# Threshold offsets in another PSUM buffer, accumulation matmuls split 4, 6, 2, scaling and proposals over other steps, 14 idle matmuls at the start

## The chip, the core and the metric

The kernel runs on one core of a Trainium2 chip. Times are device microseconds (us) of one launch, inputs and outputs in HBM. PE is the matrix engine, DVE, ACT and POOL are the vector, scalar and GpSimd engines, SP issues most DMAs. Smaller is better.

## The reference, cut to what matters

Capped attention over 8 batches, 12 heads, 448 positions, 64 channels, then a mixture of 8 experts in which tokens are given out greedily in the order of their logits, at most 448 to an expert and one expert to a token.

```python
scores = cap * np.tanh(scale * (q @ k.T) / cap)
attn = np.exp(scores - max); attn /= attn.sum(-1)
x = (attn @ v)                       # 3584 tokens of 768
flat = (x @ w_gate).flatten()        # 3584 x 8 logits
for idx in np.argsort(-flat):        # greedy, capacity 448
    tok, e = idx // 8, idx % 8
    if assigned[tok] >= 0 or counts[e] >= 448: continue
    assigned[tok] = e; counts[e] += 1
out[mask_e] = np.maximum(x[mask_e] @ w1[e], 0) @ w2[e]
```

## The kernel before, in words

**Attention** (`attention`, from line 22). Heads are worked on four at a time: 24 groups `g`, three to a batch, `b, m = divmod(g, 3)`. Step `g` computes the scores of group `g` in seven rounds of matmuls (`qk`, line 157; line 152 in the first and last group) into `psS`, of which there are two buffers. ACT takes the tanh of each (line 158) and, two or three rounds together, the exponential (line 163). In between, PE multiplies the exponentials of group `g-1` with the values (`avq`, line 197) into two buffers `psA`, which DVE copies to `xT` (`av_out`, line 218) before the next group may use them. DVE also adds the exponentials up (`esum`, line 168: four instructions a group, `et` and `es`).

The sums over positions and the gate logits of batch `bb = b-1` are accumulated one batch later by twelve small matmuls (`rnd`, line 228). Each writes 32 of the 128 partitions of one PSUM buffer, and `R[x]` says which 32 (`k`) and from what: in the order of `R`, entries 0 to 3, 4 to 7 and 8 to 11 each hold the four values of `k` once. Five of them are issued in step m=0, five in m=1, two in m=2; for batch 0 the two sums of group 0 take two matmuls each.

After the last two (m=2) DVE copies the result (`logit_in`, line 244), PE transposes it (line 250), and DVE turns it into logits (lines 265 to 270). In the last batch (b=7) the transposes (`logit(bb)`) stand right behind the copy, in front of the fifth round of scores; in the others they stand at the end of the step. `turn2` (line 235) transposes `xT` into `Y` on DVE; two batches later `inv` (line 241) and `scale` (line 35, two halves of 1344 columns) normalise `Y`, and `put` (line 32) writes it out. `propose` (lines 474 to 505, on DVE) prepares the search from the logits of two batches at a time: twelve small operations (`propose_a`) and six (`propose_b`).

Within attention PE, ACT, DVE and SP do their instructions in the order in which the code issues them; a wait stops all that stands behind it on the same engine.

**The first search** (`search`, `select`). The 448 best tokens of the first expert are found by 16 threshold steps in three runs, A (5), B (6) and C (5). A step compares all values with three thresholds, one on ACT (line 538) and two on DVE, adds the counts up by a small matmul (line 550), and picks the next threshold (line 554, `fl` and `t0`). From a run's second step on (`quick`) DVE's compare (line 542) adds the distance of the thresholds to `t0` itself; that distance is an operand in PSUM, `s.cps`, which lies in columns 128 and up of `psX`. Columns 0 to 127 of the same buffer are the target of idle matmuls (`warm`, line 786), whose result nobody reads: PE gets two, one or five of them behind each step's small matmul, and, in some steps, also a transpose of the last batch's output (line 40) or a part of the last group's product (line 209).

A tile's readers wait for its writers through semaphores that the framework places by tile.

**The experts** (`ffn_all`). From 360 us PE multiplies the gathered tokens with both weight matrices of expert after expert (lines 951 and 1013) until 834 us, with hardly a gap.

At the very start (lines 68 to 74) ACT's queue issues the load of the single number `cap`, half of the first group's `q`, and `cap` for all partitions (`capt`, from which DVE makes the `bias` of the exponential); PE does four idle matmuls.

Of the kernel before, what the change touches and what calls it, by code (L numbers as in the profile page):

```python
# [6 lines left out]
F32=mybir.dt.float32; F32R=mybir.dt.float32r; BF16=mybir.dt.bfloat16; F16=mybir.dt.float16; I32=mybir.dt.int32; I16=mybir.dt.int16  # L7
AF=mybir.ActivationFunctionType; ALU=mybir.AluOpType; AX=mybir.AxisListType
# [10 lines left out]
def attention(nc, tc, c1, xp, yp, ep, nv, pM, q, k, v, vl, cap, w_gate, xs, L1, ident, on_logits, on_turn, setup, mark):  # L19
# [11 lines left out]
    def put(b):  # L31
        for c in range(4): nc.sync.dma_start(rows(b)[:,c*W:c*W+W].rearrange("(k s) c -> s k c",s=32),Y[b][c*32:c*32+32].rearrange("p k n d -> p k (n d)"))
    def scale(b,i,eng):
        w=slice(i*NB//2,(i+1)*NB//2)
        eng.tensor_tensor(Y[b][:,w],Y[b][:,w],sm[b][:,w].unsqueeze(3).broadcast_to([128,NB//2,NP,32]),op=ALU.mult)
# [13 lines left out]
    with ExitStack() as ctx:  # L49
# [8 lines left out]
        def load(g,part,lo=0,hi=HG*S,eng=None):  # L58
            if g>=N: return
            if part==2:  # L60
                vz=nv.tile([128,7*HG*D],F32,name="nv")
                nc.sync.dma_start(vz,v[g])
                nats[g,2]=vz.rearrange("p (r h d) -> p r h d",r=7,h=HG) if whole(g) else (vz[:,:6*HG*D].rearrange("p (j h d) -> p j h d",j=3,d=D),vz[:,6*HG*D:].rearrange("p (h d) -> p h d",d=D))
                return
            if lo==0: tks[g,part]=tp.tile([128,HG,S],F32,name="t"+"kq"[part])
            (eng or nc.sync).dma_start(tks[g,part].rearrange("p m s -> p (m s)")[:,lo:hi],(k,q)[part][g][:,lo:hi])
        cap1=c1.tile([1,1],F32,name="cap1"); capt=c1.tile([128,1],F32,name="capt")
        nc.scalar.dma_start(cap1,cap)
        for part in range(2): load(0,part,0,S,(nc.sync,nc.scalar)[part])
        nc.scalar.dma_start(capt,cap.broadcast_to([128,1]))  # L70
        tb=c1.tile([128,1],F32,name="tb")
        nc.vector.memset(tb,0.0); nc.scalar.activation(tb,tb,AF.Tanh)
        ps=pM.tile([128,512],F32,name="psM")
        for _ in range(4): nc.tensor.matmul(ps[:,:128],ident,ident,start=True,stop=True)

        ones=c2.tile([128,NQ,HG,32],F32,name="ones")
        nc.gpsimd.memset(ones,0.0)
# [88 lines left out]
        def esum(g,what):  # L166
            if not 0<=g<N: return
            add=lambda o,a,b: nc.vector.tensor_tensor(o,a,b,op=ALU.add)  # L168
            if g==0:
                if what=='e1': es_t[g]=es.tile([128,2,2,S],F32,name="es0",bufs=1)  # L170
                t=es_t[g]
                if what in ('e1','e2'):
                    o=int(what[1])-1
                    add(t[:,o],ex(g,o,0),ex(g,o,1)); add(t[:,o],t[:,o],ex(g,o,2))
                else:
                    e=ev(g,6)
                    for o in range(2):
                        w=slice(64*(1-o),128-64*o)
                        add(t[w,o],t[w,o],e[w])
                return  # L180
            if what=='e1': et[g]=es.tile([128,2,2,S],F32,name="et",bufs=2)
            t=et[g]
            if what=='e1': add(t,eh[g,0],eh[g,1])
            if what=='e2': add(t,t,eh[g,2][:,0:2])
            if what=='r':
                es_t[g]=es.tile([128,2,S],F32,name="es",bufs=5)
                add(es_t[g],t[:,0],t[:,1]); add(es_t[g],es_t[g],ev(g,6))
        avp={}
        def avq(g,j,x):
# [50 lines left out]
            for c in range(4): nc.gpsimd.tensor_copy(sm[b][c*32:c*32+32],t[c//2*96:c//2*96+32,:,c//2*16:c//2*16+NP])  # L240
        def inv(b): nc.vector.reciprocal(sm[b],sm[b])
        def logit_in(b):
            lgs[b]=lgt[b]=xp.tile([128,S],F32,name="lg",bufs=1)
            nc.vector.tensor_copy(lgs[b],misc.pop(b)[:,:S])
        def logit(b,part=None,some=False,pool=None):
            if b not in lgs: logit_in(b)
# [45 lines left out]
        for g in range(N):  # L292
            b,m=divmod(g,NQ); bb=b-1
            for z in LD.get(g,()): load(int(z[0]),int(z[1]))
            if g>2:
                load(g+1,2); load(g+2,0); load(g+2,1)
            if g==2: gates()
            last=g==N-1
            if g==N-8: vload()
            if g==N-5: vgate()  # L300
            if g==N-3: vback()
            qk(g,0); qk(g,1)
            turn2(g-2)
            if b>1:
                if m==0: inv(b-2)
                if m<2: scale(b-2,m,nc.vector)
                if m==1: put(b-2)
            order=g>0; head=0<g<4
            for j in range(1 if head else 2 if order else 3): avq(g-1,j,0)
            if head: qk(g,2); avq(g-1,1,0)  # L310
            for w in ('e2','r'): esum(g-1,w)
            if not head: qk(g,2)
            if order: avq(g-1,2,0)
            if m==2 and b: rnd(bb,10,12)
            qk(g,3)
            if order: qk(g,4)
            if m==0 and b: rnd(bb,0,5)
            if m==1 and bb>=0:
                rnd(bb,5,10)
                if bb>0: on_logits(bb-1)  # L320
            if m==2 and bb>0: on_turn(bb-1)
            if m==2 and b: logit_in(bb)
            if m==2 and b==B-1: logit(bb)
            if order: qk(g,5)
            else: qk(g,4)
            avq(g-1,0,1)
            if head: qk(g,6)
            avq(g-1,1,1)
            if not order: qk(g,5); avq(g-1,2,1)
            if not head: qk(g,6)  # L330
            if order: avq(g-1,2,1)
            avq(g-1,3,1)
            if not last: esum(g,'e1')
            if g: av_out(g-1,0); av_out(g-1,1)
            if m==2 and 0<b<B-1: logit(bb)
            if m==2 and bb>=0: turnsum(bb)
        g=N-1; b=B-1
        rnd(b,0,8,8)
        logit_in(b)
        inv(b-1)  # L340
        vround(0); vround(1)
        part=logit(b,some=True,pool=pT)
        vround(2); vround(3)
        lgs[b]=xp.tile([128,S],F32,name="lg",bufs=1); ps=misc.pop(B)
        nc.vector.tensor_copy(lgs[b],ps[:,:S])
        ps=pT.tile([128,512],F32,name="psA")
        av(g,0,3,ps,3,2)
        logit(b,part)
        for j in range(3): av(g,0,j,ps,3,2)
    avs=[lambda ps,j=j: av(N-1,1,j,ps,0,3) for j in range(4)]  # L350
# [3 lines left out]
    return [lambda pool,i=i: lambda: held(i) for i in range(2)]+[lambda pool,p=p: xt(B-1,p,pool) for p in range(NP)],avs  # L354


YL=[]; YB=2
LK=(0,0,112,112,112,112,112,112); FT=2
ACF=1
LF=1  # L360
# [3 lines left out]
class Routing:  # L364
# [160 lines left out]
    def select(s,wp,Vt,ab,mid=None,post=None):  # L525
# [6 lines left out]
        for i in range(steps):  # L532
# [3 lines left out]
            with nc.allow_low_precision(reason="integers up to 256 are exact in bfloat16"):  # L536
                quick=s.cur==0 and i>0
                for k in [0] if quick else range(na,m): nc.scalar.activation(o,Vt,AF.Sign,bias=th[k],scale=-1.0,accum_out=cd[:,k:k+1])
                for k in range(1,m) if quick else range(na):
                    o=wp.tile([128,NV],BF16,name="cmpD",bufs=2)  # L540
                    if quick:
                        v.scalar_tensor_tensor(o,Vt[:,:NV],t0,s.cps[ab][:,i,k:k+1].broadcast_to([128,NV]),op0=ALU.subtract,op1=ALU.is_lt,accum_out=cd[:,k:k+1])  # L542
                        continue
                    with s.tc.issue_after(s.hold) if s.hold else nullcontext(): v.tensor_scalar(o,Vt[:,:NV],th[k],None,op0=ALU.is_lt,op1=ALU.add,accum_out=cd[:,k:k+1])  # L544
            if quick: v.tensor_scalar(H[:,i,m:2*m],C[:,i,0:m],t0,None,op0=ALU.add,op1=ALU.add,accum_out=wp.tile([128,1],F32,name="nt",bufs=2))
# [18 lines left out]
    def search(s,wp,turned=()):  # L564
        nc=s.nc; v=nc.vector
        post=None
        if s.cur==0:
            ps=s.spare(); s.cps={}; o=128
            for n in "ABC":
                S=s.steps[n]; s.cps[n]=ps[:,o:o+3*S].rearrange("p (s k) -> p s k",k=3); o+=3*S  # L570
                nc.scalar.activation(s.cps[n][:,1:],s.C[n][:,1:],AF.Copy)
        if turned:
            for h in range(s.NC//16):
                if ("VA",h) not in turned: s.turn("VA",h)
            late=[lambda: s.propose_b(s.NC-4,s.NC,PB(nc))]
            post=lambda: s.flips(s.pm.tile([128,512],F32,name="psM"))
        else: late,post=s.turns()
        yield 5
        yield from s.select(wp,s.V["VA"],"A",late,post)
# [157 lines left out]
def ffn_all(nc, tc, ctx, rt, xs, xz, yb, wg, w1, w2, out, ident, E, wp, deferred, xctx, gen, avs):  # L737
# [53 lines left out]
    while len(res)<1:  # L791
        step()
        if rt.pos=='B':
            warm(2 if UN[m] else 1 if m in AN else 5)
            if m in AN:
                put=avs.pop(0)(pa)
                if put: late.append(put)
            units(UN[m%len(UN)]); m+=1
        elif rt.pos=='A': posts()
# [285 lines left out]
def full(nc,tc,q,k,v,vl,cap,wg,w1,w2,out):  # L1085
    with ExitStack() as ctx:
# [3 lines left out]
        xz=[dr.tile([n,768],I16,name=f"xz{i}") for i,n in enumerate((512,384))]  # L1090
        yb=dr.tile([448,768],F32,name="yb")
        ident=cp.tile([128,128],F32,name="ident"); make_identity(nc,ident)
        cp.tile([128,64],F32,name="pad")
        L1=cp.tile([112,32,8],F32,name="L1")
        r=Routing(nc,cp,3584,8); r.ident=ident; r.tc=tc
        xctx=ExitStack()
# [1 line left out]
        xp=xctx.enter_context(tc.tile_pool(name="xp",bufs=2,side="right"))  # L1098
        yp=xctx.enter_context(tc.tile_pool(name="yp",bufs=YB,side="right"))
        ep=xctx.enter_context(tc.tile_pool(name="ep",bufs=2,side="right"))  # L1100
        nv=xctx.enter_context(tc.tile_pool(name="nv",bufs=5,side="right"))
        pM=xctx.enter_context(tc.tile_pool(name="pM",bufs=2,space=PSUM,side="right"))
        r.psum=lambda: pM.tile([128,512],F32,name="psM")
        turned=set()
        def on_logits(b):
            if b%2 or b==6: (r.propose if b<7 else r.propose_a)(L1,4*b-(4 if b<6 else 0),4*b+4)
        def on_turn(b):
            if b==3:
                r.turn("VA",b//4); turned.add(("VA",b//4))
        r.mark=[None]  # L1110
# [59 lines left out]
```

## Time and profile before

| what | us |
|---|---|
| three runs: median (lowest to highest) | 857.3 (856.39 to 859.15) |
| the profiled execution's own time | 856.05 |
| its span, first to last instruction | 854.3 |
| PE busy in the span | 827.7 (97%) |
| DVE, ACT, POOL busy | 595.3, 567.4, 392.5 |
| share of the last chain on PE, ACT, DVE | 87%, 6%, 2% |

The span is divided by what runs: attention to about 313 us, search and gather to about 360, the experts after that. PE's share of the chain is high in all of them, so the question in each stretch is which instruction PE waited for last, and what stood between two of its instructions. In a row of the timeline, square brackets give the idle time of the engine just before the row and who ended it.

### The profile page before, as it was taken

Reading aid. Unit: us, or ns where it says so; the run is one execution under the profiler, and the core shown is the slowest. Engines: PE = TensorE matmul, PEld = TensorE weight load, DVE = VectorE, ACT = ScalarE, POOL = GpSimd, SP = SyncE. Lnnn points to the kernel's source line nnn. Section 1 sums busy time; section 2 is a strip of 40 time slices with the busy share of each in tenths; the row PEclk is TensorE's granted clock in tenths of the full one; section 3 lists DMA queues with packets and bytes.
Section 4 is the critical chain, followed back from the end, with each engine's and each line's share of the span. In section 5 each row is a group of like instructions: output and inputs, shape, how many; then the busy total and the mean of one; then the engine's idle time right before and its main releaser. Section 6 shows DMA issues by size and latency. Waiting matters only on the chain.

```text
span 854.3 us, 16156 instructions
## 1 busy us (share of the span) xinstructions
PE 827.7 (97%) x5720; PEld 574.4 (67%) x5720; DVE 595.3 (70%) x1913; ACT 567.4 (66%) x747; POOL 392.5 (46%) x585
## 2 busy tenths in 40 slices
PE   6999999999999997899999999999999999999996
PEld 2333333333333435688888888888888899999996
DVE  2667889879888976777887977878868874352210
ACT  7999999999999964284393593665655755544500
POOL 7600000000000015284387497596486687786843
PEclk9999999999999999999999999999999999999999
DMA  6323536355654305360764886977967968958714
GB/s 232 116 108 130 146 115 194 109 153 156 190 116 145 66 1 130 121 241 17 271 204 134 250 281 220 288 233 220 278 220 216 298 207 242 335 185 259 241 65 130
DMA packets 116003, 155.10 MB, mean 182 GB/s; under 512 B 66962, under 2 KB 80498, under 8 KB 115922
## 3 DMA queue, kind: packets, MB, share of 16 engines
q1 hardware_dynamic: 108208, 124.73, 48.5%
q0 software_dynamic: 4832, 22.03, 7.6%
q10 hardware_dynamic: 2882, 7.31, 2.2%
q8 instruction: 45, 0.74, 0.4%
q14 instruction: 36, 0.29, 0.1%
HBM read 105.18 MB, written 40.60 MB: 171 GB/s over the span
## 4 chain that ended last, share of the span: by engine, by line
PE 87%; ACT 6%; DVE 2%; DMA 1%; issue 1%; POOL 1%; SPq 0%; ACTq 0%; DVEq 0%; POOLq 0%
PE psH L951 28%; PE psH L1013 25%; PE psA L197 12%; PE psS L157 12%; ACT e L158 3%; PE psM L228 3%; ACT e L163 3%; PE psX L786 2%; PE psS L152 1%; DVE cmpD L542 1%; POOL out_dram L971 1%; DVE cmpD L544 1%; PE psR L550 1%; DMA on<-yb 1%; PE psM L250 1%
## 5 line engine op out<-in xcount | busy, mean ns | idle before, releaser
L1013 PE MATMUL psH<-hh,w2h 128*128 128x448 f32 x720 | 199.2, 367 | 0.0
L158 ACT ACTIVATE e<-psS 128x896 f32<-128x896 f32 x168 | 148.0, 912 | 21.7 <-PE psS L157 17.2
L163 ACT ACTIVATE e<-e,bias 128x1792 f32<-128x1792 f32 (+2 forms) x74 | 147.1, 1990 | 0.9
L157 PE MATMUL psS<-tq,tk 64*64 64x448 f32 x1248 | 140.4, 544 | 5.7 <-ACT e L158 5.5
L951 PE MATMUL psH<-xgh,w1h 128*128 128x448 f32 (+1 forms) x384 | 141.7, 369 | 0.3 <-ACT xgh L901 0.2
L1013 PEld LDWEIGHTS psH<-hh,w2h 128*128 128x128 f32 x720 | 134.1, 188 | 8.9 <-DVE hh L961 0.6
L951 PE MATMUL psH<-xgh,w1l 128*128 128x448 f32 (+1 forms) x384 | 139.8, 364 | 0.0
L829 POOL TENSOR_TENSOR w1l<-w1r,w1h 128x768 fp32r<-128x768 f32 x62 | 115.3, 1861 | 51.6 <-ACT w1h L822 46.2
L951 PE MATMUL psH<-xgl,w1h 128*128 128x448 f32 (+1 forms) x384 | 135.6, 366 | 0.0
L829 POOL TENSOR_TENSOR w2l<-w2r,w2h 128x768 fp32r<-128x768 f32 x64 | 132.1, 2066 | 6.2 <-ACT w2h L822 4.6
L197 PE MATMUL psA<-e,nv 64*64 64x448 f32 x1232 | 132.2, 536 | 0.0
L240 POOL COPY sm<-lgt 32x84 f32<-32x84 f32 x28 | 6.9, 247 | 264.9 <-DVE lgt L238 264.1
L1013 PE MATMUL psH<-hh,w2l 128*128 128x448 f32 x360 | 124.3, 367 | 0.0
L157 PEld LDWEIGHTS psS<-tq,tk 64*64 64x64 f32 x1248 | 43.1, 132 | 85.2 <-ACT e L158 42.5
L197 PEld LDWEIGHTS psA<-e,nv 64*64 64x64 f32 x1232 | 48.6, 133 | 67.6 <-issue 64.9
L822 ACT ACTIVATE w2h<-w2r 128x768 fp32r<-128x768 f32 x64 | 76.6, 1210 | 0.3 <-DMA w2r<-in_moe_w_dram 0.2
L951 PEld LDWEIGHTS psH<-xgh,w1h 128*128 128x128 f32 x384 | 72.4, 189 | 5.7 <-ACT xgh L901 0.9
L951 PEld LDWEIGHTS psH<-xgh,w1l 128*128 128x128 f32 x384 | 72.2, 188 | 4.5
L951 PEld LDWEIGHTS psH<-xgl,w1h 128*128 128x128 f32 x384 | 72.2, 188 | 4.3 <-DVE xgl L913 0.2
L1013 PEld LDWEIGHTS psH<-hh,w2l 128*128 128x128 f32 x360 | 67.6, 188 | 4.3
L168 DVE TENSOR_TENSOR et<-e,e 128x1792 f32<-128x1792 f32 x22 | 44.5, 2022 | 34.9 <-ACT e L163 34.9
L960 ACT ACTIVATE hh<-psH 128x448 fp32r<-128x448 f32 x56 | 30.1, 538 | 58.1 <-PE psH L951 55.5
(395 smaller groups left out, 1280.6 us busy)
## 6 DMA issues: line engine op xcount, KB each, us to landing
w1r<-in_moe_w_dram SPq DMA_DIRECT2D x64, 384.0 KB, 4.8
w2r<-in_moe_w_dram SPq DMA_DIRECT2D x64, 384.0 KB, 5.6
nv<-in_v_dram SPq DMA_DIRECT2D x24, 448.0 KB, 5.6
tk<-in_k_dram SPq DMA_DIRECT2D x23, 448.0 KB, 3.4
tq<-in_q_dram SPq DMA_DIRECT2D x23, 448.0 KB, 4.7
yb<-yq SPq DMA_DIRECT2D x60, 168.0 KB, 3.8
xs<-Y SPq DMA_DIRECT2D x28, 336.0 KB, 5.8
on<-yb SPq DMA_DIRECT2D x7, 1152.0 KB
```

Of the source, the lines that this page charges most:

```text
L157: nc.tensor.matmul(ps[w:w+64,h,:S],tks[g,0][hp,o,r*64:r*64+64],tks[g,1][hp,o,:],start=True,stop=True)
L158: nc.scalar.activation(ev(g,r),ps[:,:,:S],AF.Tanh,scale=sr[0])
L163: act=lambda: nc.scalar.activation(e,e,AF.Exp,scale=sr[1],bias=bias)
L168: add=lambda o,a,b: nc.vector.tensor_tensor(o,a,b,op=ALU.add)
L197: for h in range(2): nc.tensor.matmul(avp[g,o][h*64:h*64+64,:S],z[w,r,h,:],ev(g,r)[w,h,:],start=r==0,stop=r==6)
L228: nc.tensor.matmul(ps[k*32:k*32+32,:S],lhs,rhs,start=x<4 and i==0,stop=x==max(y for y in range(end) if R[y][0]==k))
L786: for _ in range(n): nc.tensor.matmul(t[:,:128*w].rearrange("p (w c) -> p w c",w=w),ident,ident.unsqueeze(1).broadcast_to([128,w,128]),sta ...
L822: nc.scalar.activation(view(h),r,AF.Copy)
L829: (eng or nc.gpsimd).tensor_tensor(view(l),r,view(h).bitcast(F32),op=ALU.subtract)
L951: nc.tensor.matmul(ps[:,o:C],a[:,c,:],b[:,c,o:],start=(m==0 and o==0),stop=(m==DC*3-1)); m+=1
L960: nc.scalar.activation(h,ps[:,:C],AF.Relu)
L1013: nc.tensor.matmul(ps[:,:C],spl[p,2,hf,f//2][w][:,f%2,cc*128:cc*128+128],h[a][:,f],start=(m==0),stop=(m==nm-1))
```

## The change

Nine edits, all in the order and place of work; what is computed stays.

```diff
+        for part in range(2): load(0,part,0,S,(nc.sync,nc.scalar)[part])
         nc.scalar.dma_start(cap1,cap)
-        for part in range(2): load(0,part,0,S,(nc.sync,nc.scalar)[part])
...
-        for _ in range(4): nc.tensor.matmul(ps[:,:128],ident,ident,start=True,stop=True)
+        for _ in range(14): nc.tensor.matmul(ps[:,:128],ident,ident,start=True,stop=True)
...
                 if m==0: inv(b-2)
-                if m<2: scale(b-2,m,nc.vector)
-                if m==1: put(b-2)
+                if m: scale(b-2,m-1,nc.vector)
+                if m==2: put(b-2)
...
-            if m==0 and b: rnd(bb,0,5)
+            if m==0 and b: rnd(bb,0,4)
             if m==1 and bb>=0:
-                rnd(bb,5,10)
+                rnd(bb,4,10)
...
-            if m==2 and bb>=0: turnsum(bb)
+            if m==2 and 0<=bb<B-2: turnsum(bb)
...
         logit_in(b)
-        inv(b-1)
+        turnsum(b-1)
...
         av(g,0,3,ps,3,2)
+        inv(b-1)
...
-                        v.scalar_tensor_tensor(o,Vt[:,:NV],t0,s.cps[ab][:,i,k:k+1].broadcast_to([128,NV]),op0=ALU.subtract,op1=ALU.is_lt,accum_out=cd[:,k:k+1])
+                        v.scalar_tensor_tensor(o,Vt[:,:NV],t0,s.cps[ab][:,i-1,k-1:k].broadcast_to([128,NV]),op0=ALU.subtract,op1=ALU.is_lt,accum_out=cd[:,k:k+1])
...
-            ps=s.spare(); s.cps={}; o=128
+            ps=s.pm.tile([128,512],F32,name="psM"); s.cps={}; o=480
             for n in "ABC":
-                S=s.steps[n]; s.cps[n]=ps[:,o:o+3*S].rearrange("p (s k) -> p s k",k=3); o+=3*S
-                nc.scalar.activation(s.cps[n][:,1:],s.C[n][:,1:],AF.Copy)
+                S=s.steps[n]-1; s.cps[n]=ps[:,o:o+2*S].rearrange("p (s k) -> p s k",k=2); o+=2*S
+                nc.scalar.activation(s.cps[n],s.C[n][:,1:,1:],AF.Copy)
...
-            post=lambda: s.flips(s.pm.tile([128,512],F32,name="psM"))
+            post=lambda: s.flips(ps)
...
-            warm(2 if UN[m] else 1 if m in AN else 5)
+            warm(2 if UN[m] else 1 if m in AN else 4)
...
         def on_logits(b):
-            if b%2 or b==6: (r.propose if b<7 else r.propose_a)(L1,4*b-(4 if b<6 else 0),4*b+4)
+            if b%2 or b==6: r.propose_a(L1,4*b-(4 if b<6 else 0),4*b+4)
+            if b==6: r.propose_b(4*b,4*b+4)
         def on_turn(b):
+            if b%2 and b<6: r.propose_b(4*b-4,4*b+4)
```

The number of buffers follows: `Y` 2 to 3, `lg` 1 to 2, `es` 5 to 4, `nv` 5 to 4, and a pad is 8 columns smaller. `on_logits(bb-1)` is called in step m=1, `on_turn(bb-1)` in m=2.

On PE, the accumulation matmuls of one batch (steps m=0 and m=1 of a middle batch; `xT,gw` are gate entries, `es,ones` sums) stand like this before:

```order
L157 MATMUL psS<-tq,tk 64x448 x8
L228 MATMUL psM<-xT,gw 32x448 x2
L228 MATMUL psM<-es,ones 32x448 x2
L228 MATMUL psM<-xT,gw 32x448
L157 MATMUL psS<-tq,tk 64x448 x4
...
L228 MATMUL psM<-xT,gw 32x448
L228 MATMUL psM<-es,ones 32x448 x4
```

The five of m=0 stand together, and five of m=1 behind them. After the change the same place reads:

```order
L157 MATMUL psS<-tq,tk 64x448 x8
L228 MATMUL psM<-xT,gw 32x448 x2
L228 MATMUL psM<-es,ones 32x448 x2
L157 MATMUL psS<-tq,tk 64x448 x4
...
L228 MATMUL psM<-xT,gw 32x448 x2
L228 MATMUL psM<-es,ones 32x448 x4
```

The fifth small matmul has moved from the step m=0 to the step m=1, where it is the first of six.

On DVE, the last group (step 23, b=7, m=2), from the copies of `psA` to the copy `lg` for which PE's transposes wait, before:

```order
L218 COPY xT<-psA 128x448 x2
L168 TENSOR_TENSOR et<-et,e_2759 128x1792
L168 TENSOR_TENSOR es<-et 128x896
L168 TENSOR_TENSOR es<-es,e_2759 128x896
L244 COPY lg<-psM 128x448
```

Between the copies of `psA` and the copy `lg` there are three additions. After the change:

```order
L218 COPY xT<-psA 128x448 x2
L35 TENSOR_TENSOR Y<-Y,sm 128x1344
L168 TENSOR_TENSOR et<-et,e_2763 128x1792
L168 TENSOR_TENSOR es<-et 128x896
L168 TENSOR_TENSOR es<-es,e_2763 128x896
L493 TENSOR_SCALAR r_Bt<-r_b 112x8
...
L505 SCALAR_TENSOR_TENSOR r_K_348<-r_kk,r_Ct 112x8
L244 COPY lg<-psM 128x448
```

One half of a scaling (L35) and the six operations of `propose_b` now stand in front of that copy. In the other third groups they are added in the same place.

## Rows read from the trace of the kernel before

**Rows 1.** Windows of the span: each engine's busy time, granted clock, DMA share, GB/s

```profile
100.00:283.00 183.00, 181.73 (x1787) 66.62 (x1783) 156.25 (x187) 170.53 (x145) 4.94 (x20) 1.00 0.50 147
336.40:346.20 9.80, 6.30 (x52) 5.56 (x52) 5.06 (x37) 3.24 (x9) 1.08 (x2) 1.00 0.43 140
346.20:350.00 3.80, 3.80 (x20) 3.80 (x21) 2.42 (x15) 0.00 (x0) 0.00 (x0) 0.55 0.00 0
360.00:834.00 474.00, 473.38 (x2496) 424.29 (x2496) 315.77 (x1408) 264.22 (x451) 329.71 (x354) 1.00 0.70 221
```

**Rows 2.** Chain that ended last, one batch: start us, us, what

```profile
199.43 1.62 PE psM L228 x10
```

**Rows 3.** Timeline of PE, same batch: start, us, instruction, idle before

```profile
185.04 0.95 PE L228 MATMUL psM<-xT,gw 128*32 128x448 f32 x4
...
200.98 0.98 PE L157 MATMUL psS<-tq,tk 64*64 64x448 f32 x8
```

**Rows 4.** Timeline of ACT, same batch

```profile
199.74 1.72 ACT L158 ACTIVATE e<-psS 128x896 f32<-128x896 f32 x2
...
204.29 0.92 ACT L158 ACTIVATE e<-psS 128x896 f32<-128x896 f32 x1 [0.35 <-PE psS L157]
```

**Rows 5.** Timeline of DVE, a first, second and third group

```profile
190.40 2.02 DVE L168 TENSOR_TENSOR et<-e,e 128x1792 f32<-128x1792 f32 x1 [2.88 <-ACT e L163]
...
208.08 1.52 DVE L35 TENSOR_TENSOR Y<-Y,sm 128x1344 f32<-128x1344 f32 x1
...
215.40 0.17 DVE L492 TENSOR_SCALAR r_Bt<-r_b 112x8 f16<-112x8 int32 x1
...
216.04 2.02 DVE L168 TENSOR_TENSOR et<-e,e 128x1792 f32<-128x1792 f32 x1
```

**Rows 6.** Timeline of the last group, DVE and PE

```profile
294.63 1.15 DVE L218 COPY xT<-psA 128x448 f32<-128x448 f32 x2
...
296.65 2.02 DVE L168 TENSOR_TENSOR et<-et,e 128x1792 f32<-128x1792 f32 x1 [0.87 <-ACT e L163]
...
300.85 0.62 DVE L244 COPY lg<-psM 128x448 f32<-128x448 f32 x1
...
301.68 0.65 PE L250 MATMUL psM<-ident,lg 128*112 128x128 f32 x4
```

**Rows 7.** Line 542: what its engine waited for, us and times

```profile
  PE psX L786: 6.7, 13
```

**Rows 8.** Timeline of the first search, DVE and PE

```profile
327.22 0.97 PE L209 MATMUL psX<-e,nv 128*64 128x448 f32 x4
327.33 0.45 DVE L542 SCALAR_TENSOR_TENSOR cmpD<-r_qt,th,psX 128x224 bf16<-128x224 f16 x1 [0.16 <-PE psX L786]
...
332.06 0.45 DVE L542 SCALAR_TENSOR_TENSOR cmpD<-r_qt,th,psX 128x224 bf16<-128x224 f16 x1 [0.38 <-PE psX L786]
...
342.54 0.45 DVE L542 SCALAR_TENSOR_TENSOR cmpD<-r_qt,th,psX 128x224 bf16<-128x224 f16 x1 [1.05 <-PE psX L786]
...
343.46 1.36 PE L786 MATMUL psX<-ident 128*128 128x128 f32 x10
```

**Rows 9.** Timeline behind the last threshold step, PE and DVE

```profile
346.40 2.34 PE L786 MATMUL psX<-ident 128*128 128x128 f32 x10
...
347.71 0.29 DVE L657 TENSOR_TENSOR_SCAN scan<-r_ones,gteq 112x64 f16<-112x64 f16 x1
...
348.87 0.26 DVE L669 SCALAR_TENSOR_TENSOR pG<-scan,psR,gteq 112x32 f32<-112x32 f16 x1 [0.83 <-PE psR L666]
```

**Rows 10.** Timeline of the start, PE, DVE and ACT

```profile
1.53 2.08 PE L74 MATMUL psM<-ident 128*128 128x128 f32 x8 [1.53 <-POOL ident masks.py:199]
...
6.85 0.92 ACT L158 ACTIVATE e<-psS 128x896 f32<-128x896 f32 x1 [3.19 <-PE psS L152]
...
8.59 0.15 DVE L286 TENSOR_SCALAR bias<-capt 128x1 f32<-128x1 f32 x1 [6.31 <-DMA capt<-in_cap_dram]
...
9.30 1.79 ACT L163 ACTIVATE e<-e,bias 128x1792 f32<-128x1792 f32 x1
```

More of the change, by code (lines that the diff above doesn't have):

```diff
@@ L185, in esum @@
             if what=='r':
-                es_t[g]=es.tile([128,2,S],F32,name="es",bufs=5)
+                es_t[g]=es.tile([128,2,S],F32,name="es",bufs=4)
                 add(es_t[g],t[:,0],t[:,1]); add(es_t[g],es_t[g],ev(g,6))
@@ L242, in logit_in @@
         def logit_in(b):
-            lgs[b]=lgt[b]=xp.tile([128,S],F32,name="lg",bufs=1)
+            lgs[b]=lgt[b]=xp.tile([128,S],F32,name="lg",bufs=2)
             nc.vector.tensor_copy(lgs[b],misc.pop(b)[:,:S])
@@ L343, in attention @@
         vround(2); vround(3)
-        lgs[b]=xp.tile([128,S],F32,name="lg",bufs=1); ps=misc.pop(B)
+        lgs[b]=xp.tile([128,S],F32,name="lg",bufs=2); ps=misc.pop(B)
         nc.vector.tensor_copy(lgs[b],ps[:,:S])
@@ L354, in attention @@
     return [lambda pool,i=i: lambda: held(i) for i in range(2)]+[lambda pool,p=p: xt(B-1,p,pool) for p in range(NP)],avs
-YL=[]; YB=2
+YL=[]; YB=3
 LK=(0,0,112,112,112,112,112,112); FT=2
@@ L1092, in full @@
         ident=cp.tile([128,128],F32,name="ident"); make_identity(nc,ident)
-        cp.tile([128,64],F32,name="pad")
+        cp.tile([128,56],F32,name="pad")
         L1=cp.tile([112,32,8],F32,name="L1")
@@ L1100, in full @@
         ep=xctx.enter_context(tc.tile_pool(name="ep",bufs=2,side="right"))
-        nv=xctx.enter_context(tc.tile_pool(name="nv",bufs=5,side="right"))
+        nv=xctx.enter_context(tc.tile_pool(name="nv",bufs=4,side="right"))
         pM=xctx.enter_context(tc.tile_pool(name="pM",bufs=2,space=PSUM,side="right"))
```

## The prediction

> **What bounds the kernel now.** I read the windows by stage first. Between 100 and 283 us PE is busy 181.7 of 183 us and ACT 170.5: PE sets the pace of attention, with ACT 7% behind it. From 360 to 834 us PE is busy 473.4 of 474. Only in the search does everybody wait; PE is busy 6.3 of 9.8 us in its last third [rows 1]. So what the change gains has to come from less work on PE in attention, or from shorter steps of the search; the experts behind it follow as a block, since their first matmul waits only for what the search produces and for PE's own idle matmuls.
>
> Next I looked at who ended the waits of the search's compare (line 542). All of it is PE's idle matmuls: 13 times, 6.7 us together [rows 7]. Offsets and idle matmuls share the buffer `psX`, so DVE, which has a new threshold, waits until PE has finished matmuls nobody needs: 0.38 us behind two of them, 1.05 behind five, 0.16 in a step whose idle matmul stands before a piece of the last product [rows 8]. Then the chain of one batch, for the small matmuls of step m=0 (1.62 us on PE [rows 2]), and the timelines of PE, ACT and DVE around them.
>
> **The change, part by part.** The sum is made against the profiled execution (856.05 us); the median of the runs is 857.3, 1.25 above it.
>
> *Offsets in `psM`.* The 13 waits go. Nine of the steps then end on DVE's own chain (small matmul, new threshold, compare) with nothing of PE in it: two idle matmuls cost PE about 0.55 us and four about 1.1 (1.36 for five [rows 8]), and the compare alone takes two passes of 0.45. Four steps, with together 0.8 us of the waits, gain nothing, because there the product on PE (0.97 us behind the idle matmul [rows 8]) ends as late as DVE's compare. So 6.7 - 0.8 = 5.9; I take off 0.03 for each of nine handovers that stay between two DVE instructions, and 0.2 for the one step where two more matmuls stand behind the idle ones: 5.4 us gained. The bounds are 6.7 (all of it) and 3.5 (if in the four long steps, 3.9 us of the waits, PE's remaining four idle matmuls still end last, so that a little over half goes). The new neighbours in `psM` cost nothing: the transposed values `VB`, `VC` are written once, ahead of a threshold that takes longer, and the copy of `K2` by ACT happens in a step that does not read the offsets. Five idle matmuls turned into four hide behind the compare; the wait that they caused is already counted.
>
> *Behind the last step.* There PE's granted clock is 0.55 in the mean of 346.2 to 350 us, at its lower level most of the time, after a stretch in which PE was busy two thirds [rows 1]. Five idle matmuls take 2.34 us there instead of 1.36 [rows 8, 9] and PE's next useful matmul comes late: DVE has its scan ready at 348.00, and gets PE's answer at 348.87 [rows 9]. With steps about 1.0 us shorter and nearly as many idle matmuls in each, PE is busy well over 80% of the stretch ahead, and I expect no fall; then the small matmul follows the scan directly, and of the 0.87 I take 0.5 as gained. Bounds: 0.5 gained, or 0.5 lost if the clock falls a little earlier, inside the steps.
>
> *Small matmuls 4, 6, 2.* Each writes a quarter of the partitions, and four on different quarters run beside each other: the two of step m=2 take 0.95 us by the timeline [rows 3], of which the next matmul overlaps a little, and five take 1.62 [rows 2], two rounds. Four are one round, six are two rounds as five were: PE has one round, 0.75, less per batch. ACT takes part of it back: the round of scores behind the small matmuls (200.98 [rows 3]) needs the buffer that the first of two tanh frees (199.74, half of 1.72 later: 200.60 [rows 4]). One round earlier would be 200.23, so PE waits until about 200.6 and 0.4 is left; ACT, which itself waited 0.35 for PE later in that group [rows 4], moves along. That holds for batches 1 to 6. In batch 0 two sums take two matmuls each, so two rounds stay. 6 x 0.43 = 2.6 gained; bounds 0 (ACT gives nothing) and 4.5 (6 x 0.75).
>
> *Scaling and proposals a step later.* In a first group this takes 1.5 us off DVE, in a third it adds 1.5 for the scaling (1.52) and, in every second batch, 0.64 for the second part of the proposals (215.40 to 216.04) [rows 5]. In the middle batches the cover is DVE's idle time of 2.88 us ahead of the third group's `et`, which waits for ACT [rows 5]: 2.1 fit in. In the last batch nothing covers it. There the copy `lg` stands behind both, and PE's transposes stand behind the copy, ahead of PE's next scores. Before: copies end at 295.78, DVE idles 0.87 until ACT, `lg` at 300.85, transposes at 301.68 without a gap on PE [rows 6]. After: 1.52 + 0.64 more, less 0.87 of idle, is 1.3 later; and PE has nothing else to do. Loss 1.2 to 1.3; behind it everything of the last group moves along. What is queued behind the waiting transposes is PE's fifth round of scores, which ACT then waits for. Later the sum transposition and `inv` change places with copies that wait for PE; each lies in an idle time of DVE, and POOL's scaling of batch 6 does not start before the first threshold step, well after `inv`: nothing.
>
> *The buffers.* `Y` needs its third copy because a batch is now written out a step later; `es` and `nv` with four have their fourth last user a full step earlier. Nothing. SP's loads now stand ahead of the writing of `Y` that waits for DVE, and the next loads are a group away.
>
> *The start.* `q` is issued 0.5 us earlier, `cap` later, and PE does 14 idle matmuls. Four took 2.08 us, 0.52 each against 0.27 in the search [rows 8, 10], so PE was slow then. At 0.52 throughout, 14 end at 8.8 and the first exponential comes some 2.1 late; at the speed of the search, from the fifth on, they end at about 6.3, and the two tanh end at about 8.8. The first exponential waits anyway for the bias, whose input landed just before 8.59, and starts at 9.30 [rows 10]. I take 0, between 0.5 gained and 2.1 lost. The Trainium skill (TensorE: Matmul & The Clock Gate, Part 1) says that the throttled clock is the default and that activity releases it; by that the later idle matmuls run at full speed and the first scores too, and the sum stays 0 because of the bias. No run here shows 14 of them.
>
> Sum: -5.4 - 0.5 - 2.6 + 1.2 + 0 = -7.3, or 848.75 against the profiled 856.05 and 850.0 against the median. I take 849.5 between them.
>
> **The rivals.** *(a) The start costs.* `cap` is now behind 224 KB of `q` on the same queue. `capt`, which stood there before, was available only at 8.59, after DVE had waited 6.31 us [rows 10]. If `cap` comes as late, the first tanh (6.85 [rows 10]) cannot start before about 9: 2.1 lost, 851.6. For it: that one wait; against it: `capt` is 128 pieces and `cap` one. The same price holds if the idle matmuls stay slow. On the order inside a queue the Trainium skill (DMA: Bandwidth & Descriptors, Queues, rings and completion order) says that each DMA engine consumes a queue's descriptors in order; by that `cap` is late, though less than `capt`. The trace of before agrees for `capt` (8.59).
>
> *(b) ACT keeps attention where it is.* ACT is busy 93% of that stretch [rows 1]; if the round saved is given back whole at the next tanh, the -2.6 is 0 and the last group's loss stays: 852.1.
>
> *(c) The search gains less,* 3.5 instead of 5.4, and the clock still falls behind it: 2.4 less, 851.9. Against it: the row of waits names PE's idle matmuls alone.
>
> *(d) More is gained:* no give-back in attention and the last group's stall half hidden: 2.5 more, 847.0.
>
> *(e) Slower.* DVE becomes the bound in the third groups. Its work there grows by 1.5 to 2.1 us, and it decides from the point at which that no longer fits in the idle 2.88 us [rows 5], because DVE came to it late. Each of five middle batches then loses 1.5, and two of them 0.64 more, 8.8 in all, and some of it again in the group behind, where the copies of `psA` come late and PE has no buffer: about 10 us, or 859.5. Against it: DVE has less to do in the first group behind.
>
> **How the numbers follow.** Forecast 0.60, (a) 0.11, (b) 0.10, (c) 0.09, (d) 0.06, (e) 0.04. What a measurement of this kernel can tell from no change is about 0.3%, 2.6 us, so faster means under 854.7. All of the forecast, (a), (b), (c) and (d) lies there, less a few hundredths for two of them together: faster 0.92, the same 0.05, slower 0.03. The range 846.0 to 853.5 holds the forecast with its bounds and the centres of (a) to (d).
>
> **What would show it.** Right: line 542 no longer waits for line 786; the 16 threshold steps are 5 us shorter; the granted clock stays 1.00 between 336 and 350; a batch takes 0.4 us less; PE idles 1.2 us ahead of the last batch's transposes. Wrong: the first exponential later than 9.5 us; the third groups' `et` without idle time ahead of it; or the search shorter and the first matmul of the experts not earlier by the same.

## The result

| | median us (lowest to highest) | runs |
|---|---|---|
| before | 856.89 (856.39 to 859.15) | 4 |
| after | 849.65 (847.98 to 850.87) | 4 |

The ratio is 0.9909, with a 95% interval of 0.9883 to 0.9935; predicted were 849.5 and a range of 846.0 to 853.5. The profiled execution of after took 850.3 us, its span is 848.5. Lines behind attention have moved by one: the compare is line 543, the small matmul of the search 551, the idle matmuls 787.

The windows of after answer to [rows 1] (columns as there):

```profile
100.00:283.00 183.00, 179.85 (x1798) 65.89 (x1797) 158.10 (x189) 171.98 (x147) 4.94 (x20) 1.00 0.50 147
318.90:325.90 7.00, 7.00 (x28) 3.85 (x29) 3.47 (x26) 2.75 (x8) 6.07 (x6) 0.52 0.34 65
336.00:346.00 10.00, 8.06 (x67) 7.26 (x68) 8.10 (x56) 3.59 (x12) 1.38 (x3) 1.00 0.42 138
356.00:830.00 474.00, 473.55 (x2499) 424.76 (x2499) 314.18 (x1408) 264.35 (x451) 329.19 (x354) 1.00 0.70 221
```

PE is busy 8.1 of 10 us in the search's last third, where it had been 6.3 of 9.8, and the granted clock there is 1.00 to the end. New is the second row: seven microseconds at the first threshold steps with a granted clock of 0.52, where PE was at 1.00 before.

What line 543 waits for, and who waits for it (us, times), answers to [rows 7]:

```profile
  PE psM L515: 0.2, 1
...
  PEld L551: 4.4, 9
```

The 13 waits for idle matmuls are gone, and what remains of PE is 0.2 us, once. PE waits for the compare 4.4 us in nine waits, where it had been 10.9 in thirteen. Behind the last step, as in [rows 9] (timeline of DVE and PE):

```profile
344.24 0.29 DVE L658 TENSOR_TENSOR_SCAN scan<-r_ones,gteq 112x64 f16<-112x64 f16 x1
...
344.58 0.16 PE L666 MATMUL psR<-scan,r_lo 112*112 112x2 f16 x1 [0.52 <-DVE ei L660]
...
344.83 0.26 DVE L670 SCALAR_TENSOR_TENSOR pG<-scan,psR,gteq 112x32 f32<-112x32 f16 x1 [0.28 <-PE psR L667]
```

PE waits for DVE and answers 0.30 us after the scan (344.53 to 344.83), 0.87 before. In a first group, PE and ACT (beside [rows 3, 4]):

```profile
198.78 1.71 ACT L158 ACTIVATE e<-psS 128x896 f32<-128x896 f32 x2
...
199.74 0.98 PE L157 MATMUL psS<-tq,tk 64*64 64x448 f32 x8 [0.38 <-ACT e L158]
```

One round of small matmuls is gone, and in its place PE waits 0.38 us for the tanh. In the last group, DVE and PE, answering to [rows 6]:

```profile
292.66 1.16 DVE L218 COPY xT<-psA 128x448 f32<-128x448 f32 x2 [0.61 <-PE psA L197]
293.73 1.55 DVE L35 TENSOR_TENSOR Y<-Y,sm 128x1344 f32<-128x1344 f32 x1
295.20 2.02 DVE L168 TENSOR_TENSOR et<-et,e 128x1792 f32<-128x1792 f32 x1
...
300.01 0.62 DVE L244 COPY lg<-psM 128x448 f32<-128x448 f32 x1
...
300.68 0.65 PE L250 MATMUL psM<-ident,lg 128*112 128x128 f32 x4 [0.90 <-DVE lg L244]
```

DVE's idle 0.87 is filled by the scaling, and PE idles 0.90 in front of the transposes: the copies are 1.97 us earlier than before, the transposes only 1.00. At the start (beside [rows 10]):

```profile
1.53 4.94 PE L74 MATMUL psM<-ident 128*128 128x128 f32 x28 [1.53 <-POOL ident masks.py:199]
...
6.53 0.15 DVE L286 TENSOR_SCALAR bias<-capt 128x1 f32<-128x1 f32 x1 [2.21 <-DMA capt<-in_cap_dram]
...
9.20 1.79 ACT L163 ACTIVATE e<-e,bias 128x1792 f32<-128x1792 f32 x1
```

`capt` is there 2 us earlier, and the first exponential follows ACT's own two tanh.

### The profile page after: what moved, and what is told of

Read it like the earlier page. It is cut to its first block, busy times and chain, and to the rows that moved or that the text cites. A ratio compares the mean times of both kernels' runs of the same rounds, so it can differ in the third digit from the quotient of the medians.

```text
span 848.5 us, 16186 instructions
## 1 busy us (share of the span) xinstructions
PE 822.8 (97%) x5728; PEld 572.7 (67%) x5728; DVE 593.8 (70%) x1913; ACT 567.5 (67%) x747; POOL 392.9 (46%) x585
## 4 chain that ended last, share of the span: by engine, by line
PE 84%; ACT 8%; DVE 3%; issue 2%; DMA 1%; POOL 1%; SPq 0%; POOLq 0%; DVEq 0%; ACTq 0%
PE psH L952 28%; PE psH L1014 26%; PE psA L197 12%; PE psS L157 11%; ACT e L158 4%; ACT e L163 3%; PE psM L228 2%; PE psX L787 1%; POOL out_dram L972 1%; PE psX L209 1%; DVE cmpD L543 1%; PE psM L74 1%; PE psM L250 1%; DVE cmpD L545 1%; DMA on<-yb 0%
```

## The experiments

The 12 profiles of this table are cut at the same four instructions: the first copy of `psA` (line 218), the first and the last small matmul of the first search (line 550 or 551), and `pG`. "Copies" is the time from the first copy to those of the last group, ahead of its stall, against before (264.51 us); a negative number is what the text calls the lead. "Rest" is the span behind `pG`. Times are read from the timelines; medians, with the intervals of the ratio to before, are of all executions.

| kernel | to first copy | copies | first copy to first step | 16 steps | to pG | rest | median us, ratio |
|---|---|---|---|---|---|---|---|
| before | 30.12 | 0 | 288.38 | 27.24 | 3.13 | 505.4 | 856.89 |
| after | 29.99 | -1.84 | 287.52 | 24.75 | 2.57 | 503.7 | 849.65, 0.9909 [0.9883, 0.9935] |
| offsets only | 30.56 | +0.01 | 288.41 | 22.10 | 2.57 | 505.5 | 850.91, 0.9914 [0.9891, 0.9936] |
| matmuls only | 30.76 | -0.58 | 287.81 | 31.43 | 3.46 | 505.4 | 856.19, 0.9989 [0.9971, 1.0007] |
| start only | 29.95 | 0.00 | 288.40 | 27.25 | 3.45 | 506.4 | 858.61, 1.0006 [0.9991, 1.0022] |
| scaling only | 30.57 | -0.19 | 289.16 | 31.46 | 3.46 | 504.6 | 857.30, 0.9990 [0.9977, 1.0003] |
| all but scaling | 31.34 | -0.59 | 287.81 | 21.88 | 2.57 | 504.7 | 850.05, 0.9909 [0.9886, 0.9933] |
| after, again | 30.50 | -1.83 | 287.53 | 23.24 | 2.58 | 503.7 | 849.17, 0.9903 [0.9889, 0.9918] |
| bridge | 30.59 | -1.83 | 287.54 | 21.94 | 2.58 | 505.8 | 850.01, 0.9907 [0.9893, 0.9921] |
| late | 30.02 | -1.82 | 288.04 | 21.94 | 2.57 | 504.0 | 848.69, 0.9893 [0.9878, 0.9908] |
| bridge and late | 30.98 | -1.85 | 288.01 | 21.96 | 2.57 | 505.2 | 850.46, 0.9913 [0.9899, 0.9928] |
| POOL scales | 30.02 | -0.91 | 287.95 | 21.58 | 2.57 | 505.5 | 850.51, 0.9917 [0.9901, 0.9933] |

Attention repeats to 0.03 us where the code is the same, so differences of some tenths can be read there. "Late" is the run `last_group_late`, "all but scaling" is `no_scaling_move`; the other names are those of the runs below. The steps fall into groups by the clock. The start and the rest vary by 1.4 and 2.7 us with nothing to go by, and the medians with them.

**1. One part at a time.** Offsets only (`search_only`):

```diff
-            ps=s.spare(); s.cps={}; o=128
+            ps=s.pm.tile([128,512],F32,name="psM"); s.cps={}; o=480
```

> Before, with nothing but the offsets moved from psX to psM (idle matmuls stay at five). My theory: the 13 waits of the compare go, worth 5.4, and 0.5 behind the last step, so 5 to 6 us less than before, about 851.5, in executions whose TensorE clock does not fall; if the clock falls to its lower level during the first steps, as in the profiled run of after (granted 0.50 from 319 to 325 us), PE sets the pace of four steps and some 2.6 us of it are lost: about 854. Rival: the steps were worth only the 2.5 us by which the profiled run of after shortened them, whatever the clock does: 854.4 in every execution, those with a mean clock of 1.000 too.

27.24 us became 22.10, with a clock of 1.00 throughout (window from the first to the last small matmul):

```profile
318.97:341.07 22.10, 19.48 (x146) 14.16 (x147) 18.19 (x123) 13.10 (x39) 13.43 (x18) 1.00 0.50 126
```

With 0.56 behind them that is 5.7, as the theory said; the rival's 2.5 was the clock's fall in the profile of after. The medians are 7.1 apart; the 23 executions of before beside it had a lower clock more often (below).

Small matmuls only (`matmuls_only`):

```diff
-            if m==0 and b: rnd(bb,0,5)
+            if m==0 and b: rnd(bb,0,4)
-                rnd(bb,5,10)
+                rnd(bb,4,10)
```

> Before, with nothing but the small matmuls split 4, 6, 2. My theory: PE has one round less in six batches and ACT gives back 0.43 of 0.75 us each: 2.6 us less than before, and by the profile of after (PE 1.97 ahead at the last batch) rather 2.0: about 855. Rival 1, ACT keeps its pace: no change, 857. Rival 2, ACT gives all of it: 4.5 less, 852.5. The first matmul of the search tells the three apart in the profile: 318.5 in the profile of before, so 316.5, 318.5 or 314.0.

Neither the theory nor its rivals, but a value between no change and the theory: 0.58 us by the copies, 0.1 a batch. The wait for the tanh is the 0.38 of after, so at that point the gain was there. It went at the next sixteen products. The chain has 1.56 us for them in before, 1.50 in after, and here 1.87, of which it counts 15 (the timeline has all sixteen). In this order:

```profile
207.23 1.56 PE psA L197 x16
```
```profile
205.98 1.50 PE psA L197 x16
```
```profile
207.31 1.87 PE psA L197 x15
```

They need the second buffer `psA`, which DVE's copy had not emptied (timeline of DVE; its sum `et` runs right up to the copy, with no pause since 198.65):

```profile
204.31 2.02 DVE L168 TENSOR_TENSOR et<-e,e 128x1792 f32<-128x1792 f32 x1
206.25 1.15 DVE L218 COPY xT<-psA 128x448 f32<-128x448 f32 x2
```

Who waited for line 218 between 100 and 283 us (us, times), in before, with the small matmuls alone, and in after:

```profile
  PEld psA L197: 1.3, 7
```
```profile
  PEld psA L197: 3.2, 12
```
```profile
  PEld psA L197: 1.4, 9
```

The 1.9 us more in the middle one, over some five batches, are about the share of the gain that went.

Start only (`start_only`):

```diff
-        for _ in range(4): nc.tensor.matmul(ps[:,:128],ident,ident,start=True,stop=True)
+        for _ in range(14): nc.tensor.matmul(ps[:,:128],ident,ident,start=True,stop=True)
```

(with `cap` behind `q`)

> Before, with nothing but the start changed (14 idle matmuls for 4, cap issued behind q). My theory: the first exponential waits for ACT's own two tanh in place of the bias, 9.2 us in place of 9.3, so 0 to 0.1 less than before: 857. Rival: 14 idle matmuls delay the first scores and what follows, up to 2.1 more: 859. Other rival: the faster first rounds carry on through the first groups, 0.5 or more less, to be seen at the first matmul of the search, 318.5 in the profile of before.

Nothing, as forecast: 9.16 us for the first exponential, and each stretch of attention as before. But the rival's mishap occurs: in the table's eight profiles with 14 idle matmuls these took 4.90 to 6.28 us, and in the one with 6.28 the first exponential came at 10.55:

```profile
1.53 6.28 PE L74 MATMUL psM<-ident 128*128 128x128 f32 x28 [1.53 <-POOL ident masks.py:199]
```

With four it came at 9.30 to 9.95 (four profiles). On the mean, 9.6 stands against 9.7.

All but the scaling (`no_scaling_move`), that is after with these lines, and what goes with them, as in before:

```diff
-                if m: scale(b-2,m-1,nc.vector)
-                if m==2: put(b-2)
+                if m<2: scale(b-2,m,nc.vector)
+                if m==1: put(b-2)
```

> After without the move of scaling, writing out and proposals to a later step and without the buffers that it needs; offsets, small matmuls, idle matmuls and start as in after. My theory: the move only costs, 1.0 us of PE's idle time ahead of the last batch's transposes (1.2 predicted), so this is 1.0 faster than after: about 848.6. Rival: the move frees DVE in the first groups, without which the saved round of small matmuls does not come through; then PE is less than 1.97 us ahead at the last batch and the time is that of after or up to 1 us more: 849.6 to 850.6.

The rival holds: without the move the lead at the last group is 0.59, not 1.84, the same as with the small matmuls alone, and PE's waits for line 218 are 2.9 us again (11 times, in the same window). There is no stall then, and the first step comes 0.29 later than in after (287.81 against 287.52).

And the move alone (`scaling_only`): before, with the lines of the diff above the other way round.

> Before, with nothing but the scaling, writing out and proposals moved a step later (and the buffers for it). The two runs without this move (small matmuls alone, and all but this) gained 0.6 us in attention, the changed kernel 1.84 ahead of the last group's stall. My theory now: the move takes 1.5 us off DVE where DVE runs without a pause, so that its copies of psA come in time once PE is earlier; by itself, with five, five and two, it gains nothing ahead of the last group, where the copies stand within 0.1 us of before, and then costs the 1.0 us stall: 1 us more than before. Rival: the move shortens attention by itself, by 0.2 us in each of six batches: 1.2 gained at the last group's copies, and no change in all. Other rival, the prediction as I made it (moved work costs only at the end, matmuls alone gain): the same 1 us more, but then the small matmuls alone should have gained 2.6.

As the new theory said: 0.19 by the copies, then the stall (0.90, the same row as in after), and the first step 0.78 later than before.

```profile
302.91 0.65 PE L250 MATMUL psM<-ident,lg 128*112 128x128 f32 x4 [0.90 <-DVE lg L244]
```

So the two parts gain 0.57 and lose 0.78 by themselves, and together gain 0.86. What the small matmuls save came through only where DVE was 1.5 us less busy in the first groups. The move was not tested in smaller parts, the scaling without the proposals for instance.

**2. What limits the round to 0.38?** After, with shorter exponentials, at either split (`short_exp_5_5_2`, `short_exp_4_6_2`):

```diff
-            act=lambda: nc.scalar.activation(e,e,AF.Exp,scale=sr[1],bias=bias)
+            ee=e[...,:S-128]
+            act=lambda: nc.scalar.activation(ee,ee,AF.Exp,scale=sr[1],bias=bias)
```

> After with small matmuls split 5, 5, 2 again and with exponentials over 320 of 448 columns only (the other columns keep the tanh), so that ACT has about 0.5 us less to do in every two rounds. It is the measure for the next run. Both theories: PE bound as before, the copies of the last group's psA where the split 5, 5, 2 has them, within 0.3 us, since PE set the pace there.

> The same with the split 4, 6, 2. My theory: what kept the round from being worth its 0.75 us in after is ACT's tanh, for which PE waits 0.38 in every first group; with 0.5 less of exponentials that wait goes, and the split is worth 0.75 in each of six batches: 4.5 us between these two runs at the last group's copies. Rival: another engine (DVE's copies of psA) or PE itself holds the rest: about 2 us, as without the shorter exponentials.

The first half of the first expectation fell: with shorter exponentials attention gets shorter too, 286.13 us from the first copy to the first step against 289.16 with the same split in the run with the scaling alone. Of these 3.0 us 1.6 come in the first two groups and about 0.25 in each later batch, so ACT had a small share in the pace even with 5, 5, 2. The first small matmuls of the search, in the one and in the other:

```profile
314.42 0.18 PE L552 MATMUL psR<-r_cd,r_bo 128*128 128x4 bf16 x1 [1.30 <-DVE cmpD L546]
```
```profile
310.05 0.18 PE L552 MATMUL psR<-r_cd,r_bo 128*128 128x4 bf16 x1 [1.30 <-DVE cmpD L546]
```

4.37 apart, 0.13 of it from the start: 0.71 in each of six batches, nearly the whole round of 0.75. So it was ACT that kept the rest in after. (In one execution each they took 845.17 and 842.96 us; 1.27 of the lead went in the steps, 23.21 us against 21.94.)

**3. The clock.** After again (`after_again`), and with four more idle matmuls in PE's gap before the first step (`bridge`):

```diff
     warm(0)
     step()
+    warm(4)
     units(2)
```

> The changed kernel again, as the measure for the other runs beside it, and to see how often the TensorE clock falls in it: about 849.7, with a mean clock of 0.998 or more and 848 to 849 in executions without a fall at the first threshold steps, 0.996 and 850 to 851 with one (the fall cost 2.65 us of steps in its profile: 24.75 between the first and the last small matmul of the search, against 22.10 in the run with the offsets alone).

> After, with four more idle matmuls in the 1.30 us in which PE waits ahead of the first threshold step (from 316.2 us). My theory: the clock falls at 319 us because PE was busy only half of the time from 315 to 319; with the gap filled it does not fall in any execution, the slower half of the executions goes, and the median is 1 us below that of the changed kernel, about 848.5. Rival: the fall has another cause (for instance it comes from what PE does at full load before), and comes as often: no change of the median, 849.7. Other rival: the four idle matmuls end after the counts are ready and each costs the step 0.27: 0.3 to 0.5 more.

The profile of the bridge has no fall in the search, and the mean clocks of its six executions are 0.998 and 0.999 (after has 0.995 to 0.997 in five of ten). Timeline of PE, and the window of the steps:

```profile
316.67 1.12 PE L787 MATMUL psX<-ident 128*128 128x128 f32 x8
318.13 0.18 PE L551 MATMUL psR<-r_cd,r_bo 128*128 128x4 bf16 x1 [0.34 <-DVE cmpD L545]
```
```profile
318.10:340.10 22.00, 18.64 (x136) 13.14 (x137) 18.14 (x123) 13.12 (x39) 13.41 (x18) 1.00 0.50 127
```

That the idle matmuls kept the clock up is not shown. The run late (below) has the gap as it was, and its five executions have mean clocks of 0.998 to 1.000. Windows of the gap and of the stretch behind it, in after again and in late:

```profile
316.00:319.00 3.00, 1.54 (x12) 1.02 (x10) 2.38 (x17) 1.63 (x5) 2.05 (x8) 1.00 0.00 0
319.90:323.30 3.40, 3.40 (x14) 2.00 (x14) 2.04 (x14) 1.20 (x4) 3.40 (x3) 0.50 0.01 2
```
```profile
316.00:319.00 3.00, 1.53 (x12) 1.02 (x10) 2.38 (x17) 1.61 (x5) 2.03 (x8) 1.00 0.00 0
319.90:323.30 3.40, 3.26 (x25) 1.79 (x24) 2.95 (x19) 2.41 (x8) 3.40 (x3) 1.00 0.01 2
```

PE is busy 1.54 and 1.53 of the three microseconds, and only the first of the two falls. The steps of the bridge take 21.94 us, 1.30 less than in the profile of after again, but the median is not lower. In the profile the rest is 2.1 longer. A part is seen: in the third expert PE waits for its tokens, whose transposed load ended late (timeline of PE).

```profile
482.46 0.47 PE L953 MATMUL psH<-xgh,w1h 128*128 128x448 f32 x1 [0.55 <-ACT xgh L903]
```

Another 1.6 us lie behind PE's last matmul, where the outputs are written (6.9 against 5.3 us). That stretch is 5.2 to 7.4 us over the profiles, whatever was changed, so I take it for variation. A wait of PE for the third expert's tokens stands in six of the fourteen profiles, 0.23 to 1.72 us long, and not in the order in which their searches end: 1.16 with `pG` at 342.12 (POOL scales), none with `pG` at 338.93 (`short_exp_5_5_2`). So an earlier search alone does not make the load late; what does stays open.

**4. The stall in the last group.** The work moved behind the transposes (`last_group_late`), both edits together (`bridge_and_late`), or the scaling given to POOL (`pool_scale`):

```diff
+                logit(bb)
+                on_turn(bb-1); scale(b-2,1,nc.vector); put(b-2)
```
```diff
-                if m: scale(b-2,m-1,nc.vector)
+                if m: scale(b-2,m-1,nc.vector if g<N-1 else nc.gpsimd)
```

> After, with the scaling, writing out and proposals that stand ahead of the copy lg in the last group issued behind PE's transposes of it. My theory: PE's stall of 0.90 us ahead of these transposes goes and nothing takes its place: the lead of PE at the copies of the last group (1.97 us on before in the profile of after, 0.99 one group further) stays, 1.0 us less than the changed kernel, about 848.7. Rival: the moved work delays the copies of psA behind it, on which PE's next products wait, and the lead is lost there: no change, 849.7.

> Both of these edits of after together. My theory: they add up, 2 us less than the changed kernel, about 847.6, and the lowest of all. Rival: one of the two is worth nothing, then this equals the other of the two runs, 848.6.

> After, with the one scaling that stands ahead of the copy lg in the last group given to POOL, which does nothing there (0.61 us busy between 310 and 313 us, nothing before for 37 us). My theory: DVE has its 1.55 us back, PE's stall of 0.90 goes and no copy of psA comes late, as it did when that work was put behind the transposes (PE waited 1.30 for it): 1.0 us less than the changed kernel at the first small matmul of the search, about 848.2. Rival: POOL's scaling (2.43 us a half in the search) slows the DVE instructions beside it, or SP's writing out that waits for it blocks something: gain below 0.3.

None gains what was expected. Moved behind, the stall goes, but the next copies wait for the scaling, and PE's small matmuls for them:

```profile
305.12 1.55 DVE L35 TENSOR_TENSOR Y<-Y,sm 128x1344 f32<-128x1344 f32 x1
306.60 0.62 DVE L218 COPY xT<-psA 128x448 f32<-128x448 f32 x1
```
```profile
307.27 1.09 PE L228 MATMUL psM<-xT,gw 128*32 128x448 f32 x3 [1.30 <-DVE xT L218]
```

The first step is 0.52 later than in after; its lower median (848.69) goes with mean clocks of 0.998 or more in all five executions, and does not stand clear of 849.17. Both together are no better. POOL began at once, two groups early, beside DVE (timeline of both):

```profile
273.14 1.95 DVE L168 TENSOR_TENSOR et<-et,e 128x1792 f32<-128x1792 f32 x1
275.12 3.23 DVE L168 TENSOR_TENSOR es<-et 128x896 f32<-128x896 f32 x1
```
```profile
273.29 4.11 POOL L35 TENSOR_TENSOR Y<-Y,sm 128x1344 f32<-128x1344 f32 x1 [1.25 <-DVE sm L241]
```

DVE's sum took 3.23 us instead of 1.09, POOL's scaling 4.11 instead of the 2.43 of a half in the search: 0.93 of the lead is lost there, and PE still waits 0.40 for the copy `lg`. No version is clearly faster than after.

## Why the prediction was right

The time was right because two sizes were off in opposite directions, attention and the clock, and in that it was luck. By its steps:

- *Offsets.* Right, 5.4 against 5.14 (`search_only`), with five idle matmuls; 5.36 with four (all but scaling).
- *What bounds.* Right for the search, and in part wrong for attention, where "PE sets the pace": with the same work on PE and shorter exponentials it got 3.0 us shorter (289.16 to 286.13), about 0.25 a batch behind the first two groups.
- *Behind the last step.* Right, 0.5 against 0.56, and its reason fits (PE busy 81% of the stretch ahead, not "well over 80%"): in all four profiles with the offsets in `psX` the clock falls at the end of the search, in the eight with them in `psM` nowhere there.
- *The clock elsewhere* was mis-sized. The bound of 0.5 for a fall inside the steps is 2.65 in the profile of after (24.75 against 22.10) and 1.1 in the other. And before loses more than its profile shows: over the 51 executions of before beside these runs, the nine with a mean clock of 0.996 or more have a median of 855.7 us, the nine up to 0.990 one of 859.9. Among the executions at 0.998 or more the change is worth 855.3 (four of before) less 849.0 (five of after), 6.4; the terms of the table give 0.86 + 5.14 + 0.56 = 6.6, not 7.3. The rest of the measured 7.2, and of the 8.9 in the runs beside after again (858.05 to 849.17), goes with falls that come less often: 47 of the 51 executions of before are below 0.998, five of the ten of after. The mean clock is a rough measure, for it counts the whole span: offsets only has 0.997 without a fall in the search, since the clock is 0.50 behind PE's last matmuls (844 to 849 us). And of the 5.8 us by which the two profiles differ, 1.7 lie in the rest, which varies by more than that by itself.
- *Small matmuls.* The mechanism was right and the term too large: ACT takes 0.37 of 0.75, as worked out (200.23 to 200.6; PE waits 0.38). That leaves 0.38, where the prediction writes 0.4 and its sum 0.43; measured is 0.31 a batch, so 1.84 for 2.6.
- *Scaling a step later* is the step that failed, as "in a first group this takes 1.5 us off DVE", priced at nothing. It is what the gain of the small matmuls hangs on (a lead of 1.84 with it, 0.19 of that from the move alone, and 0.58 without). Its cost was right: 1.2 predicted, 0.98 measured (1.84 to 0.86).
- *Start.* 0, measured 0, within a spread that rival (a) had foreseen: not `cap`, which DVE had at 3.99 us, but idle matmuls that stay slow for up to 1.3 us longer.
- *Rivals.* (b) is out by the lead of 1.84. (c)'s fall of the clock did come, at the other end of the search. (e) was the wrong way round: DVE was at its limit in the first groups of before, and the change took work away from there; the third groups had room, 0.60 to 1.41 us of their idle time left in after.

## What to carry to other kernels

Ask of every saving on the bounding engine which engine is second, and third: here ACT took half of a round at once, and DVE, already 0.06 us late in before (1.56 against 1.50), most of what was left until it was relieved. An edit that only moves work off an engine with slack in its average may be what lets another edit pay, so the two have to be priced together. Where one buffer has readers on the critical path, keep filler work out of it.

## What the runs showed of the hardware

- The clock fell at two places of the search though PE had no pause over 1.3 us there: once PE was busy 0.21 and 0.49 of two successive microseconds ahead of it (316 to 318 us in after), and at the end after a stretch at two thirds (6.3 of 9.8 us in before). In two profiles both falls came; with the small matmuls alone the 16 steps then took 31.43 us instead of 27.24:

```profile
318.57:326.00 7.43, 6.80 (x34) 4.30 (x34) 3.56 (x26) 3.52 (x10) 6.70 (x7) 0.59 0.16 33
326.00:343.00 17.00, 13.21 (x92) 9.03 (x91) 11.78 (x78) 8.22 (x25) 6.78 (x12) 0.98 0.55 141
343.00:354.50 11.50, 9.25 (x47) 8.67 (x48) 5.25 (x37) 2.04 (x5) 0.00 (x0) 0.55 0.03 12
```

  The same code falls in one execution and not in the next, and a profile with the same pause and PE busy to the same share ahead (1.53 of 3 us against 1.54) did not fall. With four idle matmuls in the first gap no fall was seen, which is not enough to call them the reason.
- DVE's sum of two tensors and POOL's product of two ran one behind the other, not side by side: DVE 2.14 us longer, POOL 1.68. The Trainium skill (SBUF — State Buffer, Terms) says that DVE and GpSimd take a shared port pair in turns, each for a whole instruction; the trace of the POOL run agrees.
